# GateLoop attention and a maxout FFN on one core: the weights' sign carried by a negative slope, and all engine lists written anew

## The chip, the core and the metric

The kernel runs on one core of a Trainium2 chip. A core has five engines, each with its own in-order list of instructions: PE (TensorE: matmuls, and weight loads, PEld), DVE (VectorE), ACT (ScalarE), POOL (GpSimd) and SP (SyncE, which here only issues transfers). Sixteen DMA engines move data. PE writes PSUM, from which DVE and ACT read; POOL reaches SBUF alone. The metric is the device time of one execution in microseconds (us).

## What is computed

```python
def _attn_ref(q, k, v, a_re, a_im):            # (4, 8, 768, 48), float32
    mag = np.sqrt(a_re * a_re + a_im * a_im)
    scale = np.minimum(mag, 0.999) / (mag + 1e-06)
    a_re_n, a_im_n = (a_re * scale, a_im * scale)
    for t in range(S):
        new_re = ar * S_re - ai * S_im
        new_im = ar * S_im + ai * S_re
        S_re, S_im = (new_re + kv, new_im)     # kv: outer product of k and v at t
        y[:, :, t] = np.einsum('bhd,bhde->bhe', q[:, :, t], S_re)

def _moe_ref(x, w1, w2, w3, w_out):            # x: (3072, 384), from y
    h = np.maximum(np.maximum(x @ w1, x @ w2), x @ w3)
    return h @ w_out                           # d_ff = 768
```

A complex gate of modulus below one decays a state per head; the outputs go through a feed-forward layer that takes the largest of three projections. The four weight matrices arrive as 8-byte floats, since they are divided by a numpy square root; everything else is float32.

## The kernel before

The sequence of 768 steps is cut into 12 groups of 64 (g = 0 to 11). A group has two units, x and y, each with two of the four batches and all heads. Within a group the gate is turned into a log modulus and an angle (Square, Ln, Exp, Arctan on ACT, sums and products on DVE), the angle is summed along time by a matmul with a triangle (`cs`), k and q are turned by sines and cosines and scaled, transposed on PE (`tpk`, `tpq`), multiplied to masked scores (`A`, `B`), and the scores and the carried state give y. The FFN of a group then runs as differences of up-projections (`U01`, `U11`, `U02`, `U12`: half of the hidden layer, matrix; `u` takes the maximum) and a down-projection by seven products (`P1` to `P7`) on sums `S1` to `S4`.

**The order of the work is a table.** SCHEDULE (L21) is a list of words such as `turn:1`: the step `turn` of group 1. `run` (L972) maps a word to the function that emits its instructions. Class `Bound` (L189) chains every instruction to the one before it on its engine, so each engine's list follows the table literally; all instructions are emitted at L198, and the profile shows that line for nearly all of them. SLOTS (L116) gives each PSUM tile, in order of use, one of four slots (`banks`, L208). OTHER (L122) names the words that take the second of two engines: `copy` (L229) and `magnitude` (L236) on DVE in place of ACT, `increase` (L243) as an add on DVE in place of an accumulating DMA from POOL, loads of k, q and v (L370, L376) from POOL's queue in place of SP's. The three tables come from a planner that is not part of the kernel. What an instruction waits for is set by the framework from the tiles that it reads and writes, not by the tables.

**The weights.** Twelve blocks (L393) of 128 x 768 values: block 3f + m is the f-th third of w1, w2 or w3 (m = 0, 1, 2), blocks 9 to 11 are w_out. `WLi` loads block i as pairs of 32-bit words, low and high (L404); `weight_step` (L419) makes float32 of them in steps that are words too. `Wai` (ACT) takes the absolute value of the high words, times 2^-112, into a packed tile `xhx`; `Wbi` (DVE) caps it; `Wci` shifts left by three; `Wei` ors in the low words' top bits; `Wfi` puts the high words' sign bit on it and writes the block. Blocks 0, 3 and 6 (w1) come out with the opposite sign, and `Wgi` adds them onto w2 and w3, so that the up-projections give differences from w1. The high words are every second word of the raw block; `xhx` is packed. A raw block lies in another weight's tile (`w`, `wo`), in `xhx` or in `strassen` (ROOMS, L129), which is the second name on a row of these steps.

**Words that the prediction names.** `abs0`, `abs1`, `abs`: magnitude of the gate's real part (suffix 0 and 1: one unit of group 0). `pw`: PE adds two tiles into PSUM; `lnw`, `expL`: Ln and Exp of it on ACT; `mulai`: DVE multiplies by the result; `atan`, `turn`: Arctan on ACT, then the angle in turns on DVE (w<-w,ar). `T0` to `T2`, `M0` to `M2`, `m1`, `m0`: the product of w1 and w_out for the FFN's base, transposed, multiplied on PE, and copied by ACT (wo<-wm). `Qc`, `Kc`: copies of the transposed q and k; `Q1`, `Q2`, `QB`, `KB`: products with decay factors; `g0` to `g3`: masked picks of scores. `sums`, `Ek`, `Eq`, `En`: sums of the log modulus and their Exp. `F`, `f0` to `f3`: factors per block of time. `addw`, `Lnop`: accumulations, most of them as POOL's DMAs.

Of the kernel before, what the change touches and what calls it, by code (L numbers as in the profile page):

```python
# [22 lines left out]
Lnop0:0 WL0:0 sqr1:0 Wa0:0 add1:0 CL:0 lnL1:0 expe1:0 Lkx:0 abs0:0 Lix:1 Wb0:0 Wc0:0 We0:0 WL3:0 half0:0 expw1:0 Fx:0
lne1:0 relu1:0 Lnop1:0 pw0:0 Wa3:0 Wf0:0 abs1:0 Wb3:0 half1:0 WL6:0 lnw0:0 expL0:0 f3x:0 Liy:1 f2x:0 Lrx:1 Wc3:0 Wa6:0
f1x:0 Lry:1 mulai0:0 mulw0:0 We3:0 Wb6:0 WL9:0 pw1:0 lnw1:0 stt0:0 expL1:0 mulw1:0 f0x:0 atan0:0 mulai1:0 Wf3:0 T0:0
sqi:1 stt1:0 turn0:0 Wc6:0 atan1:0 Lqy:0 sumsx:0 csx:0 turn1:0 We6:0 Lqx:0 sqr:1 add:1 Wf6:0 Wa9:0 Wb9:0 WL11:0 WL10:0
xor:1 Enx:0 Eqx:0 lnL:1 Wc9:0 Ekx:0 tx:0 relu:1 mkx:0 csy:0 expe:1 We9:0 nfx:0 expw:1 sumsy:0 Lix:2 ty:0 Wf9:0 abs:1
T2:0 nfy:0 mqx:0 half:1 afx:0 Wa10:0 Wa11:0 Lvy:0 t2:0 Wb10:0 Wb11:0 Wc10:0 Wc11:0 We10:0 sax:0 We11:0 pw:1 sbx:0
uqx:0 tpqx:0 lnw:1 t0:0 Wf11:0 WL1:0 T1:0 WL2:0 Wf10:0 expL:1 Qcx:0 Lky:0 ukx:0 tpkx:0 mulw:1 Wa1:0 t1:0 Cdx:0 Lvx:0
Eqy:0 Kcx:0 Wa2:0 lne:1 Q2x:0 Fy:0 f2y:0 Wb1:0 f1y:0 WL4:0 kEnx:0 Q1x:0 M0:0 f3y:0 Liy:2 f0y:0 Eny:0 mulai:1 Wb2:0  # L30
afy:0 Ax:0 Wc1:0 stt:1 We1:0 mqy:0 Wc2:0 Wf1:0 We2:0 Eky:0 say:0 QBx:0 sqi:2 KBx:0 Lnop:1 sby:0 Wa4:0 Wf2:0 g0x:0
dkx:0 Lrx:2 Lry:2 sqr:2 add:2 atan:1 lnL:2 Wb4:0 Cdy:0 turn:1 WL5:0 Wg1:0 Wc4:0 M1:0 h1x:0 expe:2 cs:1 relu:2 g1x:0
Liy:3 expw:2 t:1 Wa5:0 abs:2 lne:2 We4:0 g2x:0 mky:0 Wf4:0 uky:0 M2:0 g3x:0 Bx:0 Wb5:0 nfx:1 Wc5:0 m1:0 Z3:0 b1x:0
tpky:0 Zh:0 uqy:0 nfy:1 b0x:0 tpqy:0 We5:0 Wg4:0 Lix:3 F:1 Kcy:0 yx:0 Lqy:1 Qcy:0 Wf5:0 xor:2 m0:0 Q2y:0 xx:0 addw:2
Q1y:0 KBy:0 WL7:0 f1:1 f0:1 QBy:0 Wg2:0 sumsx:1 Enx:1 WL8:0 half:2 Cdx:1 Ekx:1 Cdy:1 U11x:0 u11x:0 Lqx:1 lnw:2 Ay:0
Wa7:0 g0y:0 Eqx:1 expL:2 af:1 U01x:0 Wb7:0 f2:1 u01x:0 U02x:0 g1y:0 By:0 mulai:2 Wg5:0 g2y:0 Wc7:0 Wa8:0 g3y:0 We7:0
b0y:0 Lky:1 b1y:0 kEny:0 Wf7:0 sumsy:1 f3:1 yy:0 mulw:2 xy:0 sb:1 dky:0 u02x:0 stt:2 U02y:0 Lkx:1 h1y:0 Z4:0 mqx:1
atan:2 U11y:0 Lnop:2 Wb8:0 mkx:1 turn:2 sa:1 ukx:1 u11y:0 U01y:0 U12y:0 u01y:0 Eky:1 uqx:1 u02y:0 Eqy:1 cs:2 u12y:0
tpqx:1 Wc8:0 We8:0 mky:1 Eny:1 Lky:2 tpkx:1 Qcx:1 Wf8:0 t:2 Wg7:0 U21y:0 Wg8:0 U21x:0 nfy:2 nfx:2 Q1x:1 Lqx:2 mqy:1
Q2x:1 kEnx:1 uqy:1 u21y:0 U22y:0 u22y:0 u21x:0 af:2 Kcx:1 sumsx:2 F:2 Ax:1 g0x:1 g1x:1 g2x:1 Ekx:2 Enx:2 Eqx:2 Z2:0  # L40
Lvx:1 f1:2 f3:2 KBx:1 h0x:1 uky:1 tpqy:1 f2:2 Qcy:1 Q1y:1 g3x:1 Oy:0 Lvy:2 tpky:1 Q2y:1 mqx:2 Lvy:1 f0:2 Lkx:2 sa:2
sqi:3 oy:0 Lry:3 J3:0 QBx:1 dkx:1 Bx:1 sb:2 h1x:1 U12x:0 QBy:1 uqx:2 QGx:1 U22x:0 Kcy:1 KBy:1 Lrx:3 Lqy:2 u22x:0
u12x:0 Ay:1 b1x:1 g0y:1 g1y:1 g2y:1 g3y:1 b0x:1 mkx:2 sqr:3 tpqx:2 Qcx:2 By:1 yx:1 add:3 lnL:3 QBx:2 expe:3 b0y:1
sumsy:2 xx:1 Eqy:2 Eky:2 expw:3 relu:3 Q1x:2 b1y:1 QGy:1 abs:3 Ox:0 Q2x:2 Lix:4 ukx:2 ox:0 mky:2 mqy:2 Dy:0 uky:2 yy:1
addw:3 tpky:2 lne:3 kEny:1 tpkx:2 Liy:4 Lnop:3 xy:1 xor:3 half:3 Cdy:2 Kcy:2 U11:1 Cdx:2 J1:0 U01:1 Lqx:3 Lrx:4 uqy:2
lnw:3 Kcx:2 KBx:2 J2:0 expL:3 u11:1 Dx:0 Eny:2 mulw:3 mulai:3 stt:3 kEny:2 h0y:1 tpqy:2 atan:3 Lry:4 sqi:4 turn:3
Qcy:2 dky:1 h1y:1 kEnx:2 sumsx:3 u01:1 J4:0 cs:3 Eqx:3 mqx:3 Ax:2 h0y:2 Ekx:3 t:3 sqr:4 add:4 g0x:2 g1x:2 g2x:2 U12:1
Enx:3 Lrx:5 nfx:3 U02:1 lnL:4 expe:4 Q1y:2 nfy:3 expw:4 u12:1 S3:1 af:3 dky:2 g3x:2 relu:4 abs:4 addw:4 Q2y:2 F:3
u02:1 Bx:2 Ay:2 Lvx:2 sb:3 S1:1 f2:3 Lkx:3 h1y:2 f1:3 QGx:2 Lqy:3 P5:1 S2:1 P7:1 f0:3 QBy:2 g0y:2 KBy:2 g1y:2 f3:3
S4:1 lnw:4 g2y:2 P1:1 expL:4 h0x:2 P6:1 r1:1 b0x:2 b1x:2 g3y:2 r6:1 dkx:2 r5:1 r7:1 lne:4 Lry:5 sa:3 Lky:3 r57:1 h1x:2  # L50
sumsy:3 By:2 xor:4 mkx:3 b1y:2 b0y:2 Eny:3 half:4 Cdy:3 Liy:5 yx:2 xx:2 mulw:4 Eky:3 Eqy:3 Py:1 QGy:2 Px:1 P4:1 P3:1
yy:2 ukx:3 uqx:3 xy:2 oy:1 tpkx:3 tpqx:3 mky:3 h0x:3 mulai:4 Kcx:3 Lix:5 sqi:5 stt:4 Qcx:3 Lqx:4 Lky:4 P2:1 uky:3
Lnop:4 atan:4 U01:2 ox:1 u01:2 tpky:3 Lvy:3 QGx:3 Kcy:3 mqy:3 Cdx:3 uqy:3 tpqy:3 turn:4 sumsx:4 Qcy:3 Lrx:6 kEny:3
KBx:3 h0y:3 Lkx:4 Q2y:3 QBx:3 Ekx:4 Enx:4 Q1y:3 Eqx:4 cs:4 F:4 f1:4 mkx:4 t:4 sqr:5 U11:2 u11:2 Lqx:6 f3:4 Q2x:3 f2:4
Dy:1 nfx:4 Q1x:3 nfy:4 Ay:3 add:5 g0y:3 Ax:3 f0:4 g0x:3 g1y:3 g2y:3 af:4 mqx:4 xor:5 Bx:3 g3y:3 sb:4 KBy:3 U02:2 sa:4
g1x:3 U12:2 ukx:4 u02:2 S3:2 g2x:3 tpkx:4 g3x:3 Lvx:3 uqx:4 Lvy:4 lnL:5 expw:5 relu:5 Lqy:4 u12:2 expe:5 Kcx:4 tpqx:4
Qcx:4 dky:3 kEnx:3 dkx:3 S1:2 h1y:3 sumsy:4 S2:2 P5:2 h1x:3 Eqy:4 QBy:3 Dx:1 abs:5 Liy:6 addw:5 b0x:3 b1x:3 lne:5
Lnop:5 half:5 Eky:4 mky:4 Eny:4 mqy:4 Cdx:4 S4:2 Cdy:4 P1:2 P6:2 Py:2 P4:2 r1:2 yx:3 r6:2 r5:2 By:3 lnw:5 expL:5 b0y:3
mulw:5 uqy:4 h0x:4 b1y:3 mulai:5 QGy:3 Px:2 stt:5 atan:5 Lix:6 P3:2 Lry:6 xx:3 sqr:6 Liy:7 P7:2 r7:2 Lkx:5 uky:4 P2:2
tpqy:4 Lky:5 Qcy:4 r57:2 tpky:4 yy:3 sqi:6 ox:2 Lqx:5 kEnx:4 kEny:4 Lvx:4 dkx:4 oy:2 add:6 xy:3 Kcy:4 sumsy:5 turn:5  # L60
sumsx:5 h1x:4 QGx:4 Dy:2 Dx:2 Ekx:5 cs:5 Q1y:4 lnL:6 Lix:7 Eqx:5 U11:3 mkx:5 expw:6 Lvx:5 relu:6 KBx:4 Q2x:4 Enx:5
expe:6 lne:6 h0y:4 Q2y:4 mqx:5 Eky:5 U01:3 Lnop:6 abs:6 Q1x:4 u11:3 t:5 nfy:5 nfx:5 Eny:5 QBx:4 u01:3 Eqy:5 mky:5
xor:6 Ax:4 af:5 g0x:4 addw:6 sb:5 dky:4 h1y:4 sa:5 F:5 half:6 f3:5 uqx:5 g1x:4 g2x:4 lnw:6 expL:6 U12:3 u12:3 f2:5
Lrx:7 f0:5 f1:5 U02:3 tpqx:5 g3x:4 mulai:6 uky:5 tpky:5 Qcx:5 mulw:6 u02:3 Lqy:5 S1:3 Ay:4 Bx:4 S2:3 P1:3 QBy:4 sqi:7
S3:3 mqy:5 b1x:4 P5:3 Kcy:5 b0x:4 KBy:4 g0y:4 P6:3 stt:6 g1y:4 uqy:5 By:4 atan:6 yx:4 ukx:5 P7:3 g2y:4 g3y:4 Lkx:6
Lry:7 sqr:7 QGy:4 b0y:4 b1y:4 Cdy:5 Cdx:5 Q1x:5 tpkx:5 xx:4 Kcx:5 turn:6 tpqy:5 add:7 S4:3 Qcy:5 Lvx:6 r1:3 yy:4 xy:4
sumsx:6 Eqx:6 cs:6 t:6 lnL:7 r6:3 Px:3 kEnx:5 r5:3 Q2x:5 Py:3 P4:3 Enx:6 h0x:5 Ekx:6 xor:7 nfy:6 kEny:5 P2:3 U01:4
r7:3 nfx:6 expw:7 dkx:5 expe:7 lne:7 relu:7 abs:7 r57:3 addw:7 QGx:5 af:6 Lry:8 Lvy:5 h1x:5 mqx:6 sb:6 Lqy:6 u01:4
sumsy:6 QBx:5 sa:6 F:6 Liy:8 U11:4 f3:6 Eqy:6 mkx:6 Q2y:5 Eky:6 KBx:5 mqy:6 P3:3 Lky:6 Q1y:5 f1:6 uqy:6 Lrx:8 h0y:5
f0:6 oy:3 Eny:6 ox:3 Bx:5 u11:4 KBy:5 lnw:7 Ax:5 g0x:5 Ay:5 g1x:5 half:7 g2x:5 expL:7 f2:6 g3x:5 mulai:7 U02:4 g0y:5  # L70
g1y:5 g2y:5 b0x:5 g3y:5 QBy:5 b1x:5 mky:6 yx:5 ukx:6 By:5 Lvy:6 Dx:3 Cdy:6 u02:4 Cdx:6 QGy:5 mulw:7 b1y:5 uqx:6 U12:4
P1:4 S3:4 b0y:5 P7:4 stt:7 atan:7 Lqx:7 xx:5 u12:4 S1:4 tpqx:6 tpkx:6 S2:4 Kcx:6 yy:5 turn:7 Lnop:7 dky:5 Qcx:6 uky:6
Lkx:7 r1:4 sqr:8 sumsx:7 xy:5 h1y:5 cs:7 t:7 kEnx:6 Lix:8 sqi:8 P6:4 Px:4 Py:4 P5:4 P2:4 P4:4 QBx:6 Dy:3 h0x:6 add:8
lnL:8 relu:8 Q1x:6 expw:8 nfx:7 Q2x:6 Eqx:7 expe:8 S4:4 nfy:7 P3:4 tpqy:6 r6:4 KBx:6 Lqx:8 abs:8 Liy:9 r5:4 r7:4 Ekx:7
r57:4 tpky:6 ox:4 oy:4 Enx:7 af:7 dkx:6 Qcy:6 kEny:6 F:7 Dx:4 sa:7 xor:8 h1x:6 half:8 sb:7 h0y:6 Lkx:8 Dy:4 f0:7 f2:7
Q2y:6 f1:7 QGx:6 U11:5 u11:5 Cdx:7 mkx:7 U12:5 Kcy:6 u12:5 Q1y:6 Lry:9 Cdy:7 U01:5 Lrx:9 Lix:9 mqx:7 addw:8 f3:7 ukx:7
# [994 lines left out]
```

## Time and profile before

| | before |
|---|---|
| median of 3 runs (549.47 to 550.01) | 549.74 us |
| span of the profiled execution, first to last instruction | 550.3 us |
| instructions | 22368 |
| PE busy | 515.6 us, 94% of the span |
| PE weight loads | 441.4 us, 80% |
| DVE busy | 484.8 us, 88% |
| ACT busy | 363.8 us, 66% |
| POOL busy | 115.6 us, 21% |

The span is that of one profiled execution; the runs' times are taken apart from it, and their median is 0.6 us shorter. Busy shares over the whole span mix stretches with different limits. A row of a group reads: line, engine, operation, tile written <- tiles read, shapes, count | busy us, mean ns of one | idle time of its engine ahead of it and what ended that. A row of a timeline reads: start, length in us, engine, the instruction, and in brackets the idle time ahead of it. A stretch reads: bounds and length, busy us of PE, PEld, DVE, ACT and POOL with their instructions, the granted clock of PE, the share of the DMA engines, GB/s.

### The profile page before, as it was taken

To read this page: it belongs to the slowest core of one execution; us is meant where nothing else is said; L and a number is where in the kernel's file an instruction comes from. 1 tells how busy PE (TensorE), PEld (TensorE's weight loads), DVE (VectorE), ACT (ScalarE), POOL (GpSimd) and SP (SyncE) were. 2 spreads that over 40 slices of the span, in tenths; PEclk is the share of its full clock that TensorE was granted. 3 is DMA by queue.
4 is the path that set the end of the run, shared out by engine and by line. 5 is a ranking of instruction groups with operands and counts; after the bars stand their busy time and mean duration, and the time that the engine had idled before them with its cause. 6 is when DMAs were issued, how large, how long until landed. Compare 5 with 4: busy or idle time off the path is not lost.

```text
span 550.3 us, 22368 instructions
## 1 busy us (share of the span) xinstructions
PE 515.6 (94%) x9998; PEld 441.4 (80%) x9998; DVE 484.8 (88%) x735; ACT 363.8 (66%) x568; POOL 115.6 (21%) x167
## 2 busy tenths in 40 slices
...
GB/s 233 243 206 170 244 129 89 101 92 69 80 89 74 96 111 104 49 91 83 104 42 121 3 52 107 64 105 112 22 104 11 66 117 2 4 30 4 2 29 29
DMA packets 117023, 47.93 MB, mean 87 GB/s; under 512 B 103936, under 2 KB 109536, under 8 KB 116928
## 3 DMA queue, kind: packets, MB, share of 16 engines
...
q10 hardware_dynamic: 2352, 0.59, 0.5%
q14 instruction: 17, 0.14, 0.1%
...
## 4 chain that ended last, share of the span: by engine, by line
PE 71%; DVE 10%; issue 2%; ACT 1%; DVEq 0%; ACTq 0%
PE up L198 28%; PE op L198 22%; PE y L198 6%; PE tp L198 4%; PE A L198 3%; PE dk L198 3%; PE sums L198 2%; DVE atm L198 1%; PE B L198 1%; DVE Q L198 1%; PE F L198 1%; DVE QG L198 1%; PE cs L198 1%; DVE uk L198 1%; DVE xhx L198 1%
## 5 line engine op out<-in xcount | busy, mean ns | idle before, releaser
L198 PE MATMUL up<-xhx,w 128*128 128x256 f32 x792 | 177.5, 382 | 0.0
L198 PEld LDWEIGHTS up<-xhx,w 128*128 128x128 f32 x792 | 148.6, 190 | 22.4 <-DVE g L198 2.2
L198 ACT ACT_TABLE_LOAD x50 | 64.2, 1283 | 4.4 <-issue 3.6
L198 POOL DMA_DIRECT2D ar<-nf x44 | 39.9, 1297 | 77.8 <-DVE ar L198 66.7
L198 ACT COPY atm<-B 32x128 f32<-32x128 f32 x96 | 24.5, 256 | 39.4 <-DVE atm L198 24.2
L198 PE MATMUL op<-wo,xhx 128*128 128x192 f32 (+1 forms) x220 | 49.2, 362 | 0.0
L198 DVE TENSOR_TENSOR Q<-Q,f 112x1024 f32<-112x1024 f32 (+1 forms) x48 | 45.3, 951 | 0.4 <-ACT Q L198 0.2
L198 PE MATMUL y<-atm,vb 128*32 128x64 f32 x1152 | 39.4, 221 | 2.9 <-issue 2.9
L198 PEld LDWEIGHTS op<-wo,xhx 128*128 128x128 f32 x220 | 36.7, 190 | 3.3 <-issue 0.6
L198 PEld LDWEIGHTS y<-atm,vb 128*32 128x32 f32 x1152 | 33.1, 110 | 7.3 <-issue 6.2
L198 PE MATMUL y<-QG,g 112*32 112x64 f32 x1408 | 37.3, 220 | 0.5 <-issue 0.5
L198 DVE TENSOR_TENSOR ot<-ot,op 128x192 f32<-128x192 f32 (+1 forms) x67 | 27.1, 413 | 11.0 <-PE op L198 6.2
L198 DVE TENSOR_TENSOR xhx<-xhx,up 128x768 f32<-128x768 f32 x22 | 20.9, 951 | 17.9 <-PE up L198 17.9
L198 PEld LDWEIGHTS y<-QG,g 112*32 112x32 f32 x1408 | 34.6, 110 | 0.7 <-issue 0.7
L198 PE MATMUL op<-wo,strassen 128*128 128x192 f32 x176 | 34.2, 339 | 0.1
L198 POOL DMA_DIRECT2D w<-L x8 | 9.0, 1124 | 117.4 <-ACT L L198 104.8
L198 PE MATMUL op<-w,strassen 128*128 128x192 f32 x176 | 32.8, 329 | 0.0
L198 DVE COPY_PREDICATED atm<-masko,A 128x256 f32<-128x256 uint8 x72 | 31.2, 435 | 1.2
L198 PEld LDWEIGHTS op<-wo,strassen 128*128 128x128 f32 x176 | 30.0, 196 | 2.3 <-issue 0.7
L198 PE MATMUL A<-Q,K 112*32 112x80 f32 x1536 | 30.6, 234 | 0.5 <-issue 0.5
L198 PEld LDWEIGHTS op<-w,strassen 128*128 128x128 f32 x176 | 28.9, 190 | 1.9 <-ACT ot L198 0.8
L198 PEld LDWEIGHTS A<-Q,K 112*32 112x32 f32 x1536 | 27.4, 110 | 3.6 <-issue 1.4
...
## 6 DMA issues: line engine op xcount, KB each, us to landing
...
```

The lines of the kernel that those rows point to most:

```text
L198: ins = f(*a, **kw)
```

## The change

The conversion of the weights loses a step, and all three tables are replaced.

```diff
-    LAST = float(np.array(0x0FEFFFFF, dtype=np.int32).view(np.float32))
+    LAST = float(np.array(0x47EFFFFF, dtype=np.int32).view(np.float32))
...
-        if step == "a":
-            activation(out=ex.bitcast(FP), in_=high.bitcast(FP), func=AF.Abs, scale=2.0 ** -112)
-        elif step == "b":
-            dve.tensor_single_scalar(out=ex.bitcast(FP), in_=ex.bitcast(FP), scalar=LAST, op=OP.min)
+        if step == "b":
+            dve.tensor_scalar(out=ex.bitcast(FP), in0=high.bitcast(FP), scalar1=LAST, scalar2=-LAST, op0=OP.min, op1=OP.max)
+        elif step == "a":
+            activation(out=ex.bitcast(FP), in_=ex.bitcast(FP), func=AF.Prelu, alpha=-2.0 ** 32,
+                       scale=-2.0 ** -112 if i in (0, 3, 6) else 2.0 ** -112)
         elif step == "c":
-            if i in (0, 3, 6):
-                dve.tensor_scalar(out=ex, in0=ex, scalar1=3, scalar2=-0x80000000, op0=OP.logical_shift_left,
-                                  op1=OP.bitwise_or)
-            else:
-                dve.tensor_single_scalar(out=ex, in_=ex, scalar=3, op=OP.logical_shift_left)
+            dve.tensor_single_scalar(out=ex, in_=ex, scalar=3, op=OP.logical_shift_left)
         elif step == "e":
-            dve.scalar_tensor_tensor(out=ex, in0=low, scalar=29, in1=ex, op0=OP.logical_shift_right, op1=OP.bitwise_or)
-        elif step == "f":
-            dve.scalar_tensor_tensor(out=dst.bitcast(I32), in0=high, scalar=-0x80000000, in1=ex,
-                                     op0=OP.bitwise_and, op1=OP.bitwise_xor)
+            dve.scalar_tensor_tensor(out=dst.bitcast(I32), in0=low, scalar=29, in1=ex, op0=OP.logical_shift_right,
+                                     op1=OP.bitwise_or)
...
-Lix:0 sqi0:0 Zf:0 Zg:0 Lrx:0 xor0:0 sqr0:0 Liy:0 Lry:0 sqi1:0 add0:0 lnL0:0 expe0:0 expw0:0 xor1:0 lne0:0 relu0:0
+Lrx:0 Lix:0 sqr0:0 sqi0:0 Liy:0 sqi1:0 Zg:0 add0:0 lnL0:0 Zf:0 expe0:0 Lry:0 sqr1:0 expw0:0 add1:0 lne0:0 lnL1:0 xor1:0
```

Step b now comes first and caps the high words on both sides. Step a is a Prelu: a positive value is scaled as before, a negative one is multiplied by -2^32 as well, so it comes out positive with an exponent that is 32 larger. The shift by three pushes that 32 into the sign bit. With the scale's sign turned for blocks 0, 3 and 6 their sign turns too. Step f is gone, and e writes the block. The planner that makes the tables now holds that a reader of a PSUM tile awaits all writes to that tile that are listed ahead of it; this is not in the kernel's text and shows only in the order of the words. PE's instructions are the same in kind and number; DVE has 726 in place of 735, ACT 560 in place of 568 (44 table loads in place of 50); nine more loads of k, q and v (net) go through POOL's queue, and fewer through SP's.

DVE, in the first 20 us, from `abs0:0` (e<-ar) on. Second names w_116 and w_117 are raw blocks 0 and 3, w_115 is w1. Before:

```order
L198 TENSOR_SCALAR e<-ar 128x384
L198 TENSOR_SCALAR xhx<-xhx 128x768 x2
L198 SCALAR_TENSOR_TENSOR xhx<-w_116,xhx 128x768
L198 TENSOR_SCALAR ar<-ar 128x384
L198 SCALAR_TENSOR_TENSOR Ln<-L,e 128x384
L198 SCALAR_TENSOR_TENSOR w_115<-w_116,xhx 128x3x256
L198 TENSOR_SCALAR xhx<-xhx 128x768
L198 TENSOR_SCALAR ar<-ar 128x384
L198 TENSOR_SCALAR xhx<-xhx 128x768
L198 TENSOR_TENSOR ai<-ai,L 128x384
```

And now:

```order
L196 TENSOR_SCALAR e<-ar 128x384
L196 TENSOR_SCALAR xhx<-w_116 128x768
L196 TENSOR_SCALAR ar<-ar 128x384
L196 SCALAR_TENSOR_TENSOR Ln<-L,e 128x384
L196 TENSOR_SCALAR xhx<-w_117 128x768
L196 TENSOR_SCALAR e<-ar 128x384
L196 TENSOR_SCALAR xhx<-xhx 128x768
L196 TENSOR_TENSOR ai<-ai,L 128x384
L196 SCALAR_TENSOR_TENSOR w_115<-w_116,xhx 128x3x256
```

Block 0 takes three rows in place of four, b reads the raw block itself, the second unit's magnitude (e<-ar) has come over from ACT, and `mulai0` (ai<-ai,L) is three rows nearer to `abs0:0`.

ACT, around the wait for the combined weights (`m1:0`, the first row wo<-wm), at 57 to 67 us of the profile before. Before:

```order
L198 ACTIVATE w<-L 128x768
L198 ACTIVATE t<-cs 128x768
L198 ACTIVATE xhx<-xhx 128x768
L198 ACTIVATE L<-ar 128x768
L198 ACTIVATE e<-e,biases 128x768
L198 ACTIVATE wo<-wm 128x384
L198 COPY atm_105<-B 32x4x32 x4
L198 COPY K<-tp 112x2x8x64
L198 COPY Q<-tp 112x2x8x2x32
L198 ACTIVATE wo<-wm 128x768
L198 COPY xT<-y 128x384
```

And now:

```order
L196 ACTIVATE w<-L 128x768
L196 ACTIVATE Ln<-L,biases 128x768
L196 ACTIVATE wo<-wm 128x384
L196 ACTIVATE L<-ar 128x768
L196 COPY atm_105<-B 32x4x32 x4
L196 COPY Q<-tp 112x2x8x2x32
L196 ACTIVATE wo<-wm 128x768
L196 ACTIVATE xhx<-xhx 128x768
L196 COPY xT<-y 128x384
L196 ACTIVATE f_113<-F 48x8x58 x2
L196 COPY K<-tp 112x2x8x64
```

The wait for PE's product stands further ahead: `lne:2` (e<-e,biases) and `abs:2` (L<-ar), which stood before it, now follow it, and k's copy has moved behind xT.

PE, from the first cumulative sums on (`csx:0` and `csy:0`, one row), about 22 to 41 us of the profile before. Before:

```order
L198 MATMUL cs<-w,upto 64x192 x8
L198 MATMUL sums<-Ln,mid 64x192 x4
L198 MATMUL sums<-Ln,rest 64x192 x4
L198 MATMUL wt<-ident,w_115 128x128 x6
L198 MATMUL pw<-w,ident 128x384
L198 MATMUL pw<-L,ident 128x384
L198 MATMUL pw<-w,ident 128x384
L198 MATMUL pw<-L,ident 128x384
L198 MATMUL tp<-ident,uq_110 112x64 x16
L198 MATMUL wt<-ident,w_115 128x128 x6
L198 MATMUL tp<-ident,uk_107 112x64 x16
```

And now:

```order
L196 MATMUL cs<-w,upto 64x192 x8
L196 MATMUL pw<-w,ident 128x384
L196 MATMUL pw<-L,ident 128x384
L196 MATMUL pw<-w,ident 128x384
L196 MATMUL pw<-L,ident 128x384
L196 MATMUL tp<-ident,uk_107 112x64 x16
L196 MATMUL tp<-ident,uq_110 112x64 x16
L196 MATMUL wt<-ident,w_115 128x128 x12
```

The second unit's sums and a transpose of w1, which stood between the cumulative sums and `pw:1`, come later.

194 lines of the change are left out of this document (96 added, 98 removed).

## The prediction

> **What bounds the kernel now.** I read the engines' busy time by stretch first, since one share over the whole span hides that the stretches have different limits. Columns: stretch, its length, busy us (instructions) of PE, PEld, DVE, ACT, POOL, then granted clock, DMA share, GB/s.
>
> ```profile
> 0.00:20.00 20.00, 6.84 (x62) 4.21 (x62) 15.99 (x41) 14.71 (x28) 17.14 (x50) 1.00 0.93 230
> 20.00:40.00 20.00, 11.84 (x68) 6.74 (x68) 19.57 (x31) 19.64 (x28) 4.87 (x6) 0.63 0.89 234
> 40.00:62.00 22.00, 18.96 (x222) 11.19 (x220) 22.00 (x34) 20.91 (x31) 7.51 (x8) 0.87 0.90 190
> 62.00:120.00 58.00, 54.75 (x1299) 44.52 (x1299) 55.30 (x82) 48.88 (x83) 12.89 (x16) 1.00 0.63 115
> 120.00:425.00 305.00, 304.65 (x6344) 268.40 (x6342) 291.24 (x429) 225.87 (x339) 61.29 (x76) 1.00 0.41 78
> 425.00:435.00 10.00, 7.40 (x219) 6.74 (x218) 6.55 (x9) 5.85 (x12) 2.69 (x4) 0.83 0.57 102
> 435.00:530.00 95.00, 94.97 (x1706) 84.61 (x1705) 65.40 (x100) 27.63 (x51) 9.18 (x12) 1.00 0.12 28
> 530.00:551.00 21.00, 16.17 (x89) 15.00 (x87) 8.73 (x15) 0.32 (x1) 0.00 (x0) 1.00 0.08 19
> ```
>
> PE idles 24.4 us before 62 us, 3.3 us up to 120, and then 0.35 us in 305: from there PE's own work sets the time. Its idle time falls into three pieces: the front (27.6 us up to 120), one hole of 2.6 us near 430, and the tail. In the front DVE and ACT are full (19.57 and 19.64 of 20 us; 22.00 and 20.91 of 22). The end therefore moves by as much as the front lets PE's stream start earlier, unless something new stops that stream. Second, the timeline at two places where PE waits for the front:
>
> ```profile
> 51.98 0.83 ACT L198 ACTIVATE w<-w 128x768 f32<-128x768 f32 x1
> 54.00 0.97 DVE L198 SCALAR_TENSOR_TENSOR w<-w,ar 128x768 f32<-128x768 f32 x1
> 54.87 0.78 ACT L198 COPY g<-dk 112x768 f32<-112x768 f32 x1
> 55.70 1.39 PE L198 MATMUL cs<-w,upto 64*64 64x384 f32 x8 [2.90 <-ACT g L198]
> 60.10 0.93 ACT L198 ACTIVATE e<-e,biases 128x768 f32<-128x768 f32 x1
> 62.33 0.49 ACT L198 ACTIVATE wo<-wm 128x384 f32<-128x384 f32 x1 [1.30 <-PE wm L198]
> 89.87 1.22 DVE L198 TENSOR_TENSOR Q<-Q,f 112x1024 f32<-112x1024 f32 x1
> 91.23 1.31 PE L198 MATMUL A<-Q,K 112*32 112x80 f32 x64
> 92.97 0.66 PE L198 MATMUL tp<-ident,uq 64*112 64x64 f32 x16 [0.42 <-ACT E L198]
> ```
>
> Gate one: the cumulative sums `cs:1` (55.70) need `turn:1` (DVE, 54.00), and stood 2.90 us idle. Gate two: the scores `Ax:1` (91.23) start 0.14 us after `Q2x:1` ends on DVE. Behind these gates PE never catches up, so a gate that opens earlier is worth its microseconds at the end.
>
> **The change, part by part.** Prices:
>
> ```profile
> 23.02 0.95 DVE L198 SCALAR_TENSOR_TENSOR xhx<-wo,xhx 128x768 int32<-128x768 int32 x1
> 23.89 0.95 DVE L198 CUSTOM_DVE_ANT_0 L<-L,e 128x768 f32<-128x768 f32 x1
> L198 DVE TENSOR_SCALAR xhx<-xhx 128x768 f32<-128x768 f32 (+1 forms) x24 | 13.3, 566 | 0.4 <-ACT xhx L198 0.4
> L198 ACT ACTIVATE xhx<-w 128x768 f32<-128x768 f32 x4 | 3.6, 905 | 0.0
> L198 ACT ACTIVATE xhx<-xhx 128x768 f32<-128x768 f32 x4 | 3.7, 920 | 0.0
> L198 DVE TENSOR_TENSOR q<-E,q 128x384 f32<-128x384 f32 x24 | 13.2, 551 | 0.7 <-ACT E L198 0.7
> L198 DVE TENSOR_TENSOR QB<-Q,f 112x512 f32<-112x512 f32 x24 | 16.4, 685 | 0.2 <-PE B L198 0.2
> L198 DVE TENSOR_TENSOR hT<-hT,up 128x256 f32<-128x256 f32 x6 | 2.4, 416 | 0.1
> L198 ACT ACTIVATE L<-ar 128x768 f32<-128x768 f32 x8 | 6.7, 843 | 0.1
> 46.57 0.52 ACT L198 ACTIVATE af<-nf 128x384 f32<-128x384 f32 x1
> L198 ACT ACTIVATE E<-sums 128x384 f32<-128x384 f32 x48 | 22.7, 489 | 9.9 <-DVE k L198 4.9 <-PE sums L198 4.8
> L198 ACT COPY Q<-tp 112x1024 f32<-112x1024 f32 x18 | 18.3, 1017 | 3.4 <-PE tp L198 3.2
> L198 DVE COPY Q<-tp 112x1024 f32<-112x1024 f32 x6 | 7.3, 1219 | 0.4 <-PE tp L198 0.4
> L198 DVE TENSOR_SCALAR L<-ar 128x768 int32<-128x768 int32 x3 | 1.7, 556 | 1.0 <-ACT Ln L198 1.0
> L198 DVE TENSOR_SCALAR e<-ar 128x384 int32<-128x384 int32 x1 | 0.4, 410 | 0.0
> 31.62 0.35 DVE L198 TENSOR_SCALAR af<-nf 128x384 int32<-128x384 int32 x1
> L198 ACT ACT_TABLE_LOAD x50 | 64.2, 1283 | 4.4 <-issue 3.6
> ```
>
> *Step f removed*, twelve times. It is a SCALAR_TENSOR_TENSOR of 128x768; the next instruction starts 0.87 us after it (23.02 to 23.89), so each costs 0.87 us of DVE, 10.4 us in all, every one ahead of gate two and eight ahead of gate one.
>
> *Step b*, twelve times, now reads the high words (every second word) where it read a packed tile. No DVE row shows a one-source operation on such words. Lower bound: the same operation on packed words, 0.566 us. Upper bound: the two-source form, which reads such words in step e, 0.95 us. That is 0 to 0.38 us more each, 0 to 4.6 us in all. I take 0: operation, size and number of sources are those of the 0.566 row, only the step differs. *Step c* loses its second operand for three blocks, at the same price; *step e* writes elsewhere.
>
> The Trainium skill (VectorE: DVE Perf Modes, "What auto-detection actually checks") asks of the double rate for one source only that source and destination lie in SBUF, with outer sizes that are even or equal; it names no step. By that rule the extra is 0 and the sum is the one below; with the upper row in its place the gates would open only 0.5 to 1.3 us earlier. No row of this trace shows the case.
>
> *Step a* is Prelu in place of Abs, behind b instead of ahead of it: one ACTIVATE of 128x768 as before. Bounds 0.905 (Abs from strided words) and 0.920 us (from packed ones, as now); no table load comes with it: the rows for ACT go from 50 loads to 44. I take 0.92, nothing gained or lost. The six saved loads (6 x 1.283 = 7.7 us) lie behind the front, where ACT is busy 225.87 of 305 us: worth nothing there.
>
> *Work handed from ACT to DVE in the front*: one copy Q<-tp (1.02 us off ACT, 1.22 onto DVE), `abs1:0`, `abs:1`, `afy:0` (0.41, 0.56, 0.35 us on DVE) and one hidden-layer maximum, taken at the 0.42 us of the like-sized row: 2.9 us onto DVE. Off ACT go 1.02, 0.84, twice 0.52 and about 0.4: some 3 us.
>
> *The lists.* Gate one, DVE's rows ahead of it: 8 f, -7.0; 9 b, 0 to +3.4; from ACT (Q, e, L, af), +2.5; `add:2`, `mqy:0` and `QBx:0` now behind, start to start about -1.9. Sum -6.4 to -3.0. Gate two: 12 f, -10.4; 12 b, 0 to +4.6; from ACT, +2.9; a turn of q that now stands ahead and smaller rows that pass, about +0.7. Sum -6.8 to -2.2.
>
> *New waits.* `mulai0:0` needs ACT's `expL0:0`; it now stands seventh behind `abs0:0` on DVE, where it stood tenth, and `expL0:0` has an Exp of the sums ahead of it that it did not have; PE starts with `pw0:0`, then does `sumsx:0`, while T2 and `sumsy:0`, which filled PE's hole before `pw:1`, come after `tpqx:0`. I bound what DVE waits there by 0 and 1.7 us (two rows E<-sums of 0.49 on ACT and one row tp of 0.66 on PE). Queued behind `mulai0:0` is all of DVE's list, so that counts in full. ACT waits for the combined weights (`m1:0`, 62.33, idle 1.30) in both lists; it now stands ahead of `lne:2` and would only wait longer if gate one did not move: it moves with it. POOL gets more loads of k and q (120 DMA words to 129) and SP fewer; POOL is busy 4.87 of 20 us there, and the loads are issued a unit ahead of use: nothing.
>
> DVE alone, with b at 0 and 1.7 us of waits, gives -4.7 to -5.1 us at the gates; ACT, also full, is relieved by only 3. The later of the two opens a gate, so I take **-4.0 us** for the front, between 3 and 5, bounds -0.5 (b at 0.95, all waits) and -6.8.
>
> *Behind the front* PE's instructions are the same in kind and number, DVE keeps 13.8 us of slack in 120 to 425, and the tail's last seven products are the same: 0.
>
> **Sum.** On the profile's span: 550.3 - 4.0 = 546.3 us. The span is 0.6 us above the median of the runs (549.74), so 545.7 us.
>
> **The rivals.**
>
> ```profile
> 430.41 0.25 PE L198 MATMUL y<-atm,vb 128*32 128x64 f32 x2 [2.60 <-issue]
> 425.00:428.00 3.00, 2.81 (x118) 2.32 (x116) 3.00 (x5) 2.26 (x6) 2.69 (x4) 1.00 0.78 134
> 428.00:431.00 3.00, 0.59 (x40) 0.59 (x44) 0.96 (x2) 1.03 (x2) 0.00 (x0) 1.00 0.99 176
> ```
>
> 1. *The hole at 430 goes.* PE stopped for 2.60 us inside `yx:9`, waiting for no engine ("issue"), after many small matmuls and with the DMA engines 0.99 busy. I read it as instructions fetched late behind POOL's transfers. In the new list the same small matmuls meet, but POOL's `addw:11` stands behind them. If no such stop occurs: 545.7 - 2.6 = 543.1. Against it: the same words, the same traffic.
>
> 2. *More such stops, slower.* With more loads on POOL's queue, a stop may come at other y words. Each costs 2.6; one extra leaves 548.3, two pass the gain: 545.7 + 5.2 = 550.9; that is the point from which it is slower. For it: the row above. Against it: one stop in 24 y words.
>
> The Trainium skill (Runtime: NRT & Kernel Launch, "Instruction fetch mechanics") calls the refill in 16 KiB blocks mostly hidden. By that this rival adds 0; the 2.60 us row is where it was not hidden.
>
> 3. *The front stays.* The DMA engines are 0.89 to 0.93 busy up to 62 us. That is 56.2 us of full use, so the transfers leave 5.8 us of the 62 to gain and no more; a weight block that lands late would hold b, which is now the first to read it, and all of DVE's list behind it. With the lower bound's 0.5 us left: 549.2. Against it: DVE's f32 step waited 0.4 us in all.
>
> 4. *Prelu is dearer.* From a surplus of 3/12 = 0.25 us each the relief of ACT is gone; at twice 0.92 us ACT is 11 us later, less 3: 557.7.
>
> 5. *The plan's rule changes nothing.* No wait is edited, only order; then part by part the sum stands on f alone, which is how it is made. Same time as the forecast.
>
> **How the numbers follow.** Forecast with rival 5, 0.47: 545.7, its own range 543.0 to 548.6. Rival 1, 0.20. Rival 3, 0.15. Rival 2, 0.12. Rival 4, 0.06. A measurement tells 0.2% (1.1 us) from no change. Faster (below 548.6): 0.45 + 0.20 + 0.05 of rival 3 = 0.70. Same: 0.02 + 0.10 + 0.02 = 0.14. Slower: 0.10 + 0.06 = 0.16. The range goes from 542.5 (rival 1 with a little more front) to 549.8, which leaves out most of rival 2, rival 4 and the best corner of the bounds.
>
> **What would show it.** Right: PE's idle time up to 120 us falls from 27.6 to about 23.6; `turn:1` ends near 50 to 51 instead of 54.97; PE as full behind 120 as now; step b at 0.57 us, a at 0.92. Wrong: b at 0.95 (front near -2.5), ACT's Prelu above 1.1 us, DVE idle for ACT or a DMA more than 2 us before 62, "issue" stops of 2 us and more in y words, or PE waiting on DVE behind 120.

## The result, and the profile after

The kernel became slower where faster was forecast.

| | before | after |
|---|---|---|
| median of the runs taken together (4 each) | 549.88 us | 553.52 us (552.25 to 554.63) |
| ratio to before, 95% interval | | 1.0069 [1.0048, 1.0090] |
| span of the profiled execution | 550.3 us | 552.9 us (its run: 554.63) |
| PE busy | 515.6 us | 513.6 us |
| DVE busy | 484.8 us | 475.5 us |
| ACT busy | 363.8 us | 354.9 us |

The stretches of after, columns as before:

```profile
0.00:20.00 20.00, 8.35 (x62) 4.62 (x62) 14.38 (x38) 13.16 (x27) 17.14 (x51) 1.00 1.00 227
20.00:40.00 20.00, 9.83 (x68) 5.18 (x68) 19.62 (x33) 19.83 (x28) 5.44 (x7) 0.66 0.94 257
40.00:62.00 22.00, 19.27 (x343) 12.03 (x344) 21.47 (x32) 21.40 (x34) 9.23 (x11) 1.00 0.94 198
62.00:120.00 58.00, 53.20 (x1185) 44.50 (x1184) 49.79 (x77) 44.76 (x75) 14.35 (x19) 0.91 0.48 95
120.00:425.00 305.00, 301.71 (x6303) 267.05 (x6300) 283.65 (x419) 218.43 (x328) 64.00 (x80) 1.00 0.40 79
425.00:435.00 10.00, 7.90 (x229) 7.04 (x228) 7.57 (x12) 7.00 (x17) 2.36 (x3) 1.00 0.32 62
```

PE's work went from 222 to 343 matmuls in 40 to 62 us: the front did open earlier. But PE now idles 4.8 us in 62 to 120 (3.3 before) and 3.3 us in 120 to 425 (0.35 before), although DVE and ACT have less to do there. The timeline of after, at the first gate and behind it:

```profile
50.16 0.94 DVE L196 SCALAR_TENSOR_TENSOR w<-w,ar 128x768 f32<-128x768 f32 x1
51.64 0.88 PE L196 MATMUL cs<-w,upto 64*64 64x384 f32 x8
56.66 0.46 PE L196 MATMUL B<-QB,KB 112*32 112x32 f32 x32
59.46 0.89 PE L196 MATMUL F<-cuts,Ln 64*48 64x29 f32 x59
65.47 0.37 PE L196 MATMUL F<-cuts,Ln 64*48 64x29 f32 x5 [5.12 <-issue]
```

The same row of `Bx:0` in before:

```profile
62.22 0.46 PE L198 MATMUL B<-QB,KB 112*32 112x32 f32 x32
```

`turn:1` ends at 51.10 (54.97 before), `cs:1` starts at 51.64 (55.70), `Bx:0` at 56.66 (62.22). Then PE stops for 5.12 us inside `F:1`, between its 59th and 60th recorded matmul, with no engine awaited. What PE awaited without a cause in the profile, in after (waiter, cause: us in all, times, longest):

```profile
PE F L196 <- issue: 5.1, 1, 5.1
PE y L196 <- issue: 3.3, 4, 2.1
PE dk L196 <- issue: 1.8, 1, 1.8
PE op L196 <- issue: 0.4, 1, 0.4
```

That is 10.5 us, where before has 3.9. The ends of some of PE's words, from both traces, show where the time went:

| word | before | after | difference |
|---|---|---|---|
| `Bx:0` | 62.68 | 57.12 | -5.56 |
| `F:1` | 65.46 | 65.83 | +0.37 |
| `U11x:0` | 68.62 | 71.16 | +2.54 |
| `yx:1` | 109.29 | 109.76 | +0.47 |
| `P4:11` (near the end) | 546.17 | 548.56 | +2.39 |

The stop takes the front's gain whole, and up to `U11x` 2.2 us more go under the halved clock that follows it (last section). By `yx:1` the kernels are nearly level again. Then after stops for 1.77 us in `dkx:3` (188 us), 0.79 in `yy:8` (403) and 2.10 in `yx:9` (432), before for 2.60 in `yx:9` alone.

**What the stops have in common.** A row of the page, the same in both kernels but for the share (queue, kind: packets, MB, share of 16 engines):

```profile
q8 instruction: 78, 1.28, 1.0%
```

78 transfers of 16 KB for PE's 19,996 recorded rows (9,998 matmuls, 9,998 weight loads): one block per 256 rows. Counted in the trace, PE's stops of after stand at rows 947, 4243, 6023, 14937 and 16207 of its stream: 13, 20, 55 and 60 steps of 253.5 to 254.4 behind the first, so each is the border of a block (some rows are not recorded). The large stop of before stands at row 16213. In the fourteen traces of this case, 69 of the 71 stops without a cause stand at such borders, and PE's next row comes 2.2 to 3.0 us after the start of a block's transfer; the other two are of 0.31 us. The transfers of after while the block of `F:1` was awaited, in two windows, 54.50 to 63.05 us and 63.05 to 64.20:

```profile
q0 software_dynamic: 957, 1.01, 74.8%
q1 hardware_dynamic: 1227, 0.94, 40.2%
issues: line engine op xcount, KB each, median us to landing
w<-w POOLq DMA_DIRECT2D x1, 384.0 KB, 12.1
w<-L POOLq DMA_DIRECT2D x1, 384.0 KB, 10.3
ai<-in_a_im_dram SPq DMA_DIRECT2D x2, 96.0 KB, 13.9
q<-in_q_dram POOLq DMA_DIRECT2D x2, 96.0 KB, 11.6
k<-in_k_dram SPq DMA_DIRECT2D x2, 96.0 KB, 11.8
```

```profile
q0 software_dynamic: 90, 0.20, 84.8%
q1 hardware_dynamic: 256, 0.05, 34.8%
q8 instruction: 1, 0.02, 5.0%
```

The shares of POOL's queue (q0) and SP's (q1) add up to over 100% of the sixteen engines, and no instruction block moved for 8.5 us. The block began at 63.11, PE had met the border at 60.35, and the row behind it came at 65.47, 2.36 us after the block's start. PE had entered the block before it near 54.8 us; at most borders of this trace the next block starts within about 2 us of such an entry, here after 8.3.

Before has a border at the same place of `F:1`, and no stop there: PE entered the block ahead of it near 60.5 us, the next block began at 62.44, and PE passed the border at 65.2. POOL's accumulations around it differ. The first that POOL of before issues behind 50.8 us, and the one in after that meets the block:

```profile
60.50 0.88 POOL L198 DMA_DIRECT2D w<-L  x1 [5.59 <-ACT L L198]
```

```profile
54.14 1.26 POOL L196 DMA_DIRECT2D w<-w  x1 [2.06 <-DVE w L196]
```

The second is `Wg4`. Before names `Wg4` and `addw:5` in OTHER, as adds on DVE; the new table makes both POOL's transfers, and makes adds of `Wg7`, `addw:8` and `addw:9`. So the nine more transfers of POOL are ten more loads and one accumulation fewer, not nine loads. `addw:5` goes out at 181.69 us, ahead of the stop in `dkx:3`; in before POOL issues nothing from 166.9 to 188.6 us, and PE passes that border, at 184.5, without a stop.

**Theory B**: PE's next block is asked for when PE enters the one before; full DMA engines start it late; a run of small matmuls uses up its 256 rows first. (When a block is asked for is not in the trace; only its transfer is.) **Rival W**: `F:1` awaits a slot or data that the profile does not name. **Rival C**: the conversion or the lists are slower in themselves.

### The profile page after: what moved, and what is told of

Read it like the earlier page. It is cut to its first block, busy times and chain, and to the rows that moved or that the text cites. A ratio compares the mean times of both kernels' runs of the same rounds, so it can differ in the third digit from the quotient of the medians.

```text
span 552.9 us, 22343 instructions
## 1 busy us (share of the span) xinstructions
PE 513.6 (93%) x9998; PEld 441.7 (80%) x9998; DVE 475.5 (86%) x726; ACT 354.9 (64%) x560; POOL 119.8 (22%) x176
## 3 DMA queue, kind: packets, MB, share of 16 engines
q8 instruction: 78, 1.28, 1.0%
## 4 chain that ended last, share of the span: by engine, by line
PE 82%; ACT 7%; DVE 5%; issue 3%; DMA 2%; ACTq 0%; SPq 0%; DVEq 0%
PE up L196 33%; PE op L196 23%; PE y L196 7%; PE A L196 5%; PE tp L196 4%; PE dk L196 4%; PE sums L196 3%; PE F L196 1%; DMA ar<-in_a_re_dram 1%; PE B L196 1%; PE cs L196 1%; ACT L L196 1%; ACT xhx L196 1%; DVE uk L196 1%; DMA ai<-in_a_im_dram 1%
## 5 line engine op out<-in xcount | busy, mean ns | idle before, releaser
L196 POOL DMA_DIRECT2D ar<-nf x44 | 41.2, 1486 | 82.1 <-DVE ar L196 56.5
L196 DVE TENSOR_TENSOR Q<-Q,f 112x512 f32<-112x512 f32 (+1 forms) x48 | 45.1, 951 | 2.1 <-ACT Q L196 2.1
L196 POOL DMA_DIRECT2D k<-in_k_dram x24 | 19.1, 896 | 53.8 <-DVE uk L196 53.8
L196 ACT ACTIVATE E<-sums 128x384 f32<-128x384 f32 x48 | 23.0, 492 | 11.9 <-PE sums L196 5.9
L196 ACT COPY xhx<-y 128x384 f32<-128x384 f32 x17 | 8.0, 478 | 34.7 <-PE y L196 27.6
```

The source lines that it names most:

```text
L196: ins = f(*a, **kw)
```

## The experiments

Ratios are to before, each with runs of before on the same chip (medians there 549.2 to 552.4 us).

| run | kernel | median, us | ratio, 95% interval |
|---|---|---|---|
| e1_shift48 | after, 24 matmuls ahead | 564.34 | 1.0287 [1.0251, 1.0322] |
| e2_shift256 | after, 128 matmuls ahead | 562.67 | 1.0225 [1.0191, 1.0258] |
| e3_convert | before's tables, new conversion | 556.62 | 1.0128 [1.0088, 1.0167] |
| e4_adds | after, two adds on DVE | 552.32 | 1.0037 [1.0000, 1.0074] |
| e5_loads | after, three loads later | 550.99 | 0.9996 [0.9970, 1.0022] |
| e6_adds5 | after, five adds on DVE | 549.54 | 0.9969 [0.9946, 0.9993] |
| e7_both | e5 and e6 together | 546.82 | 0.9920 [0.9891, 0.9950] |
| e8_before_adds | before, two adds on DVE | 548.83 | 0.9955 [0.9937, 0.9974] |
| e9_f_back | e7, step f put back | 555.16 | 1.0075 [1.0051, 1.0100] |
| e10_six | after, 6 matmuls ahead | 559.64 | 1.0134 [1.0099, 1.0168] |
| e11_both_six | e7, 6 matmuls ahead | 554.53 | 1.0041 [1.0017, 1.0065] |
| e12_six_adds | e11, two more adds on DVE | 550.43 | 0.9988 [0.9970, 1.0006] |

**Moving the borders.** Ahead of the first `pw0`, into its tile:

```diff
                 ps = T["pw", g, lo] = banks("pw")
+                for _ in range(24 if once("pads", lambda: [g]) else 0):
+                    mm(out=ps[0:32, 0, 0:64], lhsT=ident[:, 0:32], rhs=ident[:, 0:64], start=True, stop=True)
+                T["pads"].clear()
```

> The changed kernel with 24 small matmuls put ahead of everything on PE, where it idles 9.8 us anyway (their result is overwritten). Theory B, blocks of instructions: PE's rows arrive in blocks of 16384 bytes, 256 rows each; the stop of 5.12 us in the middle of the 64 matmuls of F:1 is the border of one block, whose transfer began at 63.11 us because the DMA engines were full. With 48 rows ahead of it every border moves 48 rows forward; the border that asks for this block is then crossed at about 48.0 us in place of 54.8, before the transfers pile up. The stop in F:1 falls under 0.5 us, F:1 ends near 61, and the time falls by 4 to 6 us from 553.5, to 547.5 to 549.5, if no other border is hit worse. Rival W, F:1 waits for a slot or for data that the profile does not name: the stop stays at 5 us and the time at 553 to 554.

> The control: 128 small matmuls in place of 24, 256 rows, one whole block, so every border falls on the same word as in the changed kernel. Theory B: the stop in F:1 is back at 4 to 6 us and the time at 553 to 555. If it is not the place of the borders but PE being warm or busy early that helped, or nothing helps, the time equals that of the kernel with 24 matmuls.

`F:1` in the run with 24 ran without a stop, from 59.14 on, and ended at 60.06 in place of 65.83; what PE awaited without a cause in that run:

```profile
59.14 0.92 PE L196 MATMUL F<-cuts,Ln 64*48 64x29 f32 x64 [0.15 <-ACT atm L196]
```

```profile
PE B L196 <- issue: 4.3, 5, 1.2
PE F L196 <- issue: 1.9, 1, 1.9
PE up L196 <- issue: 1.0, 1, 1.0
PE A L196 <- issue: 0.7, 2, 0.5
```

That speaks against rival W, since nothing that `F:1` needs was changed. But the time missed the expectation by 15 us. The stops had moved to other words (`B`, another `F`, `up`, `A`), all at steps of 254 rows, and the expectation had the shift wrong: the 24 matmuls show as 48 rows of PE and 48 weight loads, so words moved by 96 rows. The profiled execution was the fastest of five (558.23); what the slower ones (to 566.5) met is not known.

The control missed too. The timeline of its first work on PE:

```profile
7.35 15.90 PE L196 MATMUL pw<-ident 128*32 128x64 f32 x256 [7.35 <-POOL ident L196]
23.18 0.91 PE L196 MATMUL pw<-w,ident 128*128 128x384 f32 x2
```

128 matmuls did not fit into the 9.8 us in which PE idled; `pw0` came at 23.18 in place of 9.81, and the front up to `F:1` 9.7 us later, its transfers with it (`Wg4` at 63.86 in place of 54.14, the gate's loads at 64.01 in place of 54.29). The border in `F:1` thus met the traffic of after, with the DMA engines as full (1.18 from 62.0 to 64.9 us; after has 1.21 from 52.9 to 54.8). Still its block began at 64.91, within 0.4 us of PE's entry near 64.6, and the stop did not return. Theory B does not explain that, and so the missing stop in the run with 24 does not show by itself that the border was its cause. Three of the four other stops came back at the same words, two whole blocks further on in PE's stream: `op` 0.80 us, `dkx:3` 1.76, `yx:9` 2.04; the one in `yy:8` (0.79) did not.

**The conversion alone**, in the lists of before (words Wa and Wb change places, Wf is dropped; the first line that changes):

```diff
-Lnop0:0 WL0:0 sqr1:0 Wa0:0 add1:0 CL:0 lnL1:0 expe1:0 Lkx:0 abs0:0 Lix:1 Wb0:0 Wc0:0 We0:0 WL3:0 half0:0 expw1:0 Fx:0
+Lnop0:0 WL0:0 sqr1:0 Wb0:0 add1:0 CL:0 lnL1:0 expe1:0 Lkx:0 abs0:0 Lix:1 Wa0:0 Wc0:0 We0:0 WL3:0 half0:0 expw1:0 Fx:0
```

> The lists, slots and engine choices of before with the new conversion alone: b ahead of a, no f. If the earlier front comes from the removed step f: turn:1 ends 3 to 5 us earlier than 54.97, the time falls to 545 to 547.5 unless a border of PE's blocks is hit. If the new lists made the front earlier and the conversion is worth nothing: turn:1 stays near 55 and the time at 549.9. If the conversion is what makes the kernel slower: 552 or more.

`cs:1` started at 60.77, 5.1 us later than in before. The longest of DVE's waits in its first 62 us:

```profile
DVE xhx L198 <- ACT xhx L198: 4.3, 5, 1.8
```

ACT's step now stands between two steps of DVE, where before it stood ahead of all of them; in lists made for the old order, DVE waits for it. So the conversion without lists made for it does not pay; that this wait alone makes the 1.3% is not shown.

**Thinning the traffic.** Two accumulations as adds on DVE (names added to OTHER); three loads later (parts of the lines that change); five adds; both:

```diff
+Wg4:0 addw:2
```

> The changed kernel with two accumulations of 384 KB, Wg4 and addw of group 2, as adds on DVE in place of POOL's transfers, which are under way from 54 to 69 us. Theory B with full DMA engines as the cause of the late block: the block's transfer begins before 60 us in place of 63.11 and the stop in F:1 falls below 2.5 us; DVE has 1.9 us more to do in the full front; time 549.5 to 552. Rival W: the stop stays at 5 us, and the time becomes 554 to 556 by DVE's extra work.

```diff
-Q1y:0 tpky:0 Q2y:0 Wc5:0 f2:1 U11x:0 Lqx:1 addw:2 Wb7:0 half:2
+Q1y:0 tpky:0 Q2y:0 Wc5:0 f2:1 U11x:0 addw:2 Wb7:0 half:2
...
-Cdx:1 Lqy:1 g2y:0
+Cdx:1 Lqx:1 Lqy:1 g2y:0
...
-stt:2 yy:0 Liy:4 Lkx:1 h1y:0
+stt:2 yy:0 h1y:0
...
-sb:1 WL8:0 U11y:0
+sb:1 WL8:0 Liy:4 Lkx:1 U11y:0
```

> The changed kernel with three loads of its front issued later and nothing else moved: the gate's Liy of group 4 and Lkx of group 1 behind the last raw weight block on SP, Lqx of group 1 behind the zero rows of group 1 on POOL. They are six transfers of 96 KB in small pieces, issued from 54.3 to 58.3 us in the changed kernel, in front of the late block of PE's instructions. Theory B, the border in F:1 stops PE because the block's transfer stands in full DMA engines: the transfer begins before 60.5 us in place of 63.11, the stop in F:1 falls from 5.1 to below 2.5 us, the time to 549 to 551.5. If only the accumulations crowd it out and the loads do not: the stop stays above 4 us and the time at 552 to 554.

```diff
+Wg4:0 addw:2 addw:5 Lnop:10 addw:11
```

> The changed kernel with five of POOL's accumulating transfers as adds on DVE: Wg4 and addw of group 2 in the front, addw of group 5, Lnop of group 10 and addw of group 11 behind it. Each of the last three is issued some 5 us ahead of one of the stops at 188, 403 and 432 us. Theory B: the stops at these three fall from 1.77, 0.79 and 2.10 us to below 0.6 each, the one in F:1 to about 2.8 as in the run with two adds; DVE has 4.8 us more to do, 2.9 of them where it has slack; the time falls to 547 to 549.5. If these stops belong to the words and not to the transfers, they stay, and the time is that of the run with two adds, 552.

> Both edits together. Theory B: no stop above 1 us is left in the words F:1, dkx:3, yy:8 and yx:9, PE keeps most of the 5.6 us that the front opens earlier, and the time is 544.5 to 547. If the stops only move to other borders, as they did in the run with 24 small matmuls: the sum of the stops stays at 8 us or more and the time at 551 to 554.

The border in `F:1`, in the timelines of the runs with two adds, with loads later, with five adds, and with both:

```profile
63.21 0.28 PE L197 MATMUL F<-cuts,Ln 64*48 64x29 f32 x5 [2.81 <-issue]
```

```profile
63.85 0.30 PE L196 MATMUL F<-cuts,Ln 64*48 64x29 f32 x5 [2.37 <-issue]
```

```profile
60.13 0.88 PE L197 MATMUL F<-cuts,Ln 64*48 64x29 f32 x64
```

```profile
61.81 0.28 PE L197 MATMUL F<-cuts,Ln 64*48 64x29 f32 x5 [1.28 <-issue]
```

| run | block starts | PE at the border | next row | stop |
|---|---|---|---|---|
| after | 63.11 | 60.35 | 65.47 | 5.12 |
| e4_adds | 60.59 | 60.39 | 63.21 | 2.81 |
| e5_loads | 61.57 | 61.49 | 63.85 | 2.37 |
| e6_adds5 | 53.98 | not stopped | | 0 |
| e7_both | 59.28 | 60.53 | 61.81 | 1.28 |

PE meets the border within 1.2 us of the same time in each; the stop follows the block's start, and the row comes 2.3 to 2.6 us after that. This is where rival W falls: the end of the stop goes with the block, at four different starts of it. With two adds the block began at 60.59 and the stop was 2.81, a little over the 60 and 2.5 expected; with later loads it began at 61.57, where before 60.5 was expected. By the times, the loads alone help (0.9996 against the 1.0069 of after, the intervals apart); two adds alone are not told apart from after (1.0037, up to 1.0074).

The block's start in `F:1` is not set by the traffic alone. The runs with two and with five adds have the same lists up to `addw:5`, issued at about 180 us, yet the block began at 60.59 in one and at 53.98 in the other, 1.3 us ahead of PE's entry. What starts this one late in some executions is open.

Behind the front the stops repeat. `dkx:3` stopped for 1.76 to 1.84 us in the five profiles of the new lists that have a border there and `addw:5` on POOL (after, e2, e4, e5, e10), and for 0 to 0.45 in the five with it on DVE (e6, e7, e9, e11, e12); `yx:9` for 2.04 to 2.48 and for 0.73 to 1.13 in the same two groups, which differ in `addw:11` too. Five adds took the stops in `dkx:3` and `yy:8` to nothing; what is left without a cause in that run, and all that the DMA engines carried in its window 418 to 424:

```profile
PE y L197 <- issue: 1.1, 2, 0.7
```

```profile
DMA packets 1, 0.02 MB, mean 3 GB/s; under 512 B 0, under 2 KB 0, under 8 KB 0
...
q8 instruction: 1, 0.02, 0.9%
```

Even with the engines free of all else, `yx:9` stopped for 0.73 us: the block began at 420.91 and the row came at 423.16. So a stop in small matmuls can remain that traffic does not make. With both edits the time is 546.82 us, under both kernels; that profile has 2.5 us of stops left, of which `F:1` has 1.28, where none above 1 us was expected. (The profile with five adds was its fastest run, 545.73, and that with later loads its slowest, 555.19; medians are those of the table.)

Set against after word by word, this profile shows where the time comes from. Its lead is nothing up to the border in `F:1` (-0.2 us), 6.1 at the end of `U11x:0` (65.10 against 71.16), 5.7 from 80 to 145 us, 6.1 from 150 to 180, 4.5 ahead of `dkx:3`, 6.1 behind it, 6.5 from 300 to 400, 7.5 behind `yy:8`, and 8.6 from `yx:9` to the end; the spans differ by 8.6 (552.9 and 544.3). It grows only at stops of after and under the halved clock behind the first. At `dkx:3` nothing is gained on balance: ahead of it PE loses as much as the stop took (1.7 us), 1.14 of it in a wait for DVE.

**The same in the kernel before:**

```diff
+addw:11 Lnop:11
```

> The kernel before with two of POOL's accumulating transfers as adds on DVE, addw and Lnop of group 11, issued at 424.4 and 426.4 us, ahead of its stop of 2.60 us in yx:9. Theory B: the stop falls below 0.6 us, and the time from 549.2 to 546.5 to 548. If the stop is no matter of the transfers: it stays at 2.6 us and the time at 549 to 551.

```profile
PE y L199 <- issue: 1.2, 3, 0.7
PE F L199 <- issue: 0.6, 1, 0.6
```

The stop of 2.60 us in `yx:9` fell to 0.68, where at most 0.6 was expected, and the time by 0.45%, 2.5 us, where 1.2 to 2.7 was. The median, 548.83, lies above the 546.5 to 548 expected, on a chip where before takes 551.36. The hole at 430 was a late block too.

**What step f is worth**, put back in a form that changes no bit; its twelve words stand right behind `We`:

```diff
+        elif step == "f":
+            dve.scalar_tensor_tensor(out=dst.bitcast(I32), in0=high, scalar=0, in1=dst.bitcast(I32),
+                                     op0=OP.bitwise_and, op1=OP.bitwise_xor)
```

> The kernel with both edits (loads later, five adds on DVE), and step f put back twelve times right behind e, as an operation of its old form and size that changes no bit of the block. It prices the removed step where the stops are small. The prediction's step, DVE's list sets the front: eight of them stand ahead of gate one and twelve ahead of gate two, so at 0.87 to 0.95 us each cs:1 starts 7 to 7.6 us later and the stream behind gate two 9 to 11 us later; the time goes from 546.8 to 554 to 558. Rival, the weights' steps lie beside waits of PE for ACT and for transfers: cs:1 moves by less than 3 us and the time by less than 4.

The timeline of that run, and the group of three of its twelve steps in DVE's list:

```profile
57.52 0.88 PE L197 MATMUL cs<-w,upto 64*64 64x384 f32 x8 [0.77 <-DVE w L197]
```

```profile
L197 DVE SCALAR_TENSOR_TENSOR w<-w,w 128x768 int32<-128x768 int32 x3 | 2.9, 958 | 0.1
```

`cs:1` starts at 57.52 against 51.84 without f: 5.7 us, less than the 7 expected of eight steps; `Bx:0` comes 7.0 us later. `yx:1` ends 11.2 us later, but part of that is no matter of f: this profile ran at half clock from 65.5 to 75.7 us, that of both edits did not. The ratio rises from 0.9920 to 1.0075, some 8.5 us. The removed step did set the front, and rival C falls as far as it says that the conversion costs time.

**A shift of 24 rows, and a stop foretold.**

> The changed kernel with 6 small matmuls ahead in place of 24. The profile of the run with 24 showed 48 rows of PE and 48 weight loads for them, so that one shifted the words by 96 rows, not 48; six shift them by 24. Counted in the changed kernel's trace, the stretches between two borders (every 254 recorded rows) that PE passes in under 3.6 us are 14 unshifted, 22 with 96 rows, 11 with 24, and the border ahead of the one in F:1 is crossed near 52 us in place of 54.8. Theory B: the run with 24 was slow because of the place of the borders, not because of matmuls put ahead; with six the kernel is far from its 564 us, and the block of F:1 is asked for earlier: 549 to 552.5. If matmuls put ahead are what costs: 554 or more.

> The same six matmuls ahead of the kernel with both edits (loads later, five adds on DVE). In its trace the short stretches are 14 unshifted and 11 with 24 rows. Theory B: 544.5 to 547.5, no slower than without them, stops of PE below 2.5 us in sum. If the matmuls ahead cost: 549 or more.

Both expectations failed by some 7 us, and the times are those that were forecast on record for the rival, that matmuls put ahead cost (554 or more, 549 or more). `F:1` ran through in both, but a stop of 2.55 and 2.85 us appeared in `P7:1`, which had none (the first of the two also kept the stops behind the front: 9.4 us in all). Here it is in the run of both edits with six matmuls, and in the last run, where the two accumulations ahead of it are adds:

```profile
141.21 1.10 PE L197 MATMUL op<-w,strassen 128*128 128x192 f32 x5 [2.85 <-issue]
```

```diff
+addw:4 Lnop:4
```

> The kernel with both edits and six matmuls ahead had one large stop left, 2.85 us in P7 of group 1 at 141 us, a word that had none before: a border has moved there, and its block's transfer began at 139.0 us, while two of POOL's accumulating transfers issued at 132.3 and 134.3 us (addw and Lnop of group 4) and four loads kept the DMA engines full. Here these two are adds on DVE. Theory B: the block's transfer begins at least 1.5 us earlier, the stop in P7 falls below 1.3 us, and the time by 1.5 to 4 us from 554.5, to 550.5 to 553. If the stop belongs to the word or to the border alone: it stays above 2 us and the time at 554 to 556.5 with DVE's 1.9 us.

```profile
139.75 0.97 PE L198 MATMUL op<-w,strassen 128*128 128x192 f32 x5 [0.66 <-issue]
```

The block began at 137.48 in place of 139.00, as foretold, the stop fell to 0.66, and the ratio from 1.0041 to 0.9988 (550.43 us, the low end of what was expected). That is the test that theory B could most easily have failed: the border, its word and the two transfers were named from one trace ahead of the run. It takes back 0.0053 of the 0.0121 by which the six matmuls had raised the ratio over that of e7. Counting short stretches between borders, by which six matmuls should have done no harm, told nothing: what lies on the DMA engines at each border is needed too. The last run stays 0.7% behind e7 with like stops in its profile (2.9 us against 2.5); for this 0.7% the rival, that matmuls put ahead cost, is not excluded.

## Why the prediction was wrong

**Right: the front.** Gate one was to open 4.0 us earlier with `turn:1` ending at 50 to 51; it ended at 51.10, and `cs:1` started 4.06 us earlier. `Bx:0` gained 5.56 us on the profile of before. One caution: the run of before with two adds, whose front was not edited, reached `Bx:0` at 60.06, so between executions that point moves by 2 us, and the gain lies between 3.4 and 5.6. Both waited 2.9 us for ACT ahead of `cs:1`; in the profile of before the granted clock was 0.50 for the 3.4 us behind that wait (55.9 to 59.3), in the other 1.00. The groups of the conversion in after:

```profile
L196 DVE TENSOR_SCALAR xhx<-w 128x768 f32<-128x768 f32 x4 | 3.1, 779 | 0.0
L196 DVE TENSOR_SCALAR xhx<-xhx 128x768 f32<-128x768 f32 x4 | 2.2, 550 | 0.0
L196 DVE TENSOR_SCALAR xhx<-strassen 128x768 f32<-128x768 f32 x3 | 1.7, 553 | 0.2 <-DMA strassen<-in_moe_w_dram 0.2
L196 DVE TENSOR_SCALAR xhx<-wo 128x768 f32<-128x768 f32 x1 | 0.5, 548 | 0.0
L196 ACT ACTIVATE xhx<-xhx 128x768 f32<-128x768 f32 x12 | 9.9, 836 | 0.3 <-DVE xhx L196 0.3
```

Step b reads every second word at 0.55 us in eight of twelve, as taken, and at 0.78 in the four on `w`; in all 7.5 us against 6.8. The rule of the Trainium skill (VectorE: DVE Perf Modes, "What auto-detection actually checks"), which names no step as a condition, agrees with the eight. Prelu took 0.836 us where 0.92 was taken; rival 4 is out.

**Wrong: "the loads are issued a unit ahead of use: nothing".** The step costed the moved transfers by their own readers, and left two out: `Wg4` and `addw:5`, which went from DVE to POOL. The three loads of e5 show what it missed. In before they go out behind 65 us; the new list issued them from 54.3 to 58.3, two on SP's queue and one on POOL's, as in before. Issued later again, they took the ratio from 1.0069 to 0.9996, 0.73% or 4.0 us. From 50 us on no engine of after waited for one of them; they made something else late. That this is the block of `F:1` is likely and not shown: the profile of e5 is of its slowest run. Five accumulations as adds and the loads together took it to 0.9920. Rival 3 had seen that the DMA engines were 0.89 to 0.93 busy, and looked for the harm in a weight block.

**Wrong: "Behind the front ... 0", and PE's idle time of 23.6 us up to 120.** That idle time became 29.4. PE's own stream is the same in kind and number, and the borders of its four large stops lie in words of the same kind in before (`F`, `dk`, y, y); what moved is the traffic around them. The stops went from 3.9 to 10.5 us.

**Mis-sized: rival 2.** More such stops was the mechanism, with 2.60 us each and 0.12 chance, from "one stop in 24 y words". The size is no constant: 0.2 to 5.1 us, by how late the block starts. And the count was of the wrong thing: not y words but 78 borders, any of which can fall into small matmuls (stops came in `F`, `dk` and `op` as well as y). The profile of before held what was needed: the 2.60 us row, the 78 transfers, and POOL's transfers ahead of it.

The Trainium skill (Runtime: NRT & Kernel Launch, "Instruction fetch mechanics") gives 16 KiB blocks of 256 instructions; the 78 transfers agree. That crossing a border is "mostly hidden" holds for most of the 78; in after, five or more were not, and they decided the sign.

Three things stay open: what starts the block of `F:1` late in some executions of the same front and not in others, which fits the wider spread of some kernels (548.22 to 556.43 with two adds); what the 24-matmul kernel met in its slower runs; and the 0.7% of the last run. That late blocks decided the sign rests on the word-by-word lead of e7 over after, and on the stops behind the front, not on the runs with matmuls put ahead.
